# Places of the q, k, v weight buffers in SBUF: k-blocks padded to 1280 and 1536 bytes, operands of TensorE at multiples of 256 bytes

## The chip, the cores and the metric

The kernel runs on one core of a Trainium2 chip. The metric is the device time of one execution in microseconds; the median of several runs is compared. A profile is one more execution, taken by the hardware profiler. It has its own span (first to last instruction) and its own time.

## The reference

x has S = 2048 rows of D = 640. After a layer norm, xn goes two ways: a sliding, dilated attention (32 heads of 20, a window of 8 positions at distance 2), and a bilinear feed-forward part with F = 1536. The output is x plus the product of both, the second one through a SiLU.

```python
qkv = xn @ wqkv                                   # 640 x 1920
idx = pos[:, None] - (arange(8) * 2)[None, :]     # positions s, s-2, ..., s-14
logits = where(idx >= 0, q . k[idx], -1e9) * 20 ** -0.5
s = (softmax(logits) . v[idx]) @ wo               # 640 x 640
g = silu(((xn @ w_gate) * (xn @ w_up)) @ w_down)  # 640 x 1536, 640 x 1536, 1536 x 640
out = x + s * g
```

## The kernel before

Matrix products keep float32 accuracy by splitting each operand into a high part (rounded to TensorE's fp32r) and a low part (the rest), and adding three products: high by high, high by low, low by high. A split (function `split`, lines 84 to 87) is a copy on ScalarE that makes the high part (line 86) and a subtraction on GpSimd or VectorE that makes the low part (line 87).

SBUF buffers are made by `st(shape, tag, bufs)`. All buffers of a tag share the same one to four places, sized by the largest; places follow one another in the order in which tags are first used, each at a multiple of 32 bytes. `skip(n)` takes n bytes and does nothing else: it only shifts what comes after it.

First half, up to about 554 us of the span. The 2048 rows are 16 tiles of 128; the normed and transposed x (`xc`, high and low, four chunks of 512 columns) stays in SBUF. Two kinds of work alternate on TensorE in an order written out by hand:

- `qkv(u, i)` (line 317): a unit u is one group of heads (5, 5, 5, 5, 6, 6) and one of the two residues of the dilation, so 12 units of 8 tiles. A call has 15 matmuls: 5 k-blocks, three times. A tile of x is the stationary operand, a k-block of the group's q, k, v weights the moving one: 3 × 100 = 300 columns for the groups of 5 heads, 3 × 120 = 360 for those of 6. Weights of a group are loaded into `wraw` and split into `wqh` and `wql` by `split_wq`, one place each for all groups. ScalarE evicts k and v into `kv` (line 319) and q into `q` (line 320). At the end of tiles 4 and 7, SP copies rows of kv from each partition to the next (line 324), the halo that the window needs.
- `gate_up(f, ch)` (line 96, by `mm3`): for 128 columns of w_gate and w_up and a chunk of 512 rows, 15 matmuls of 512 columns each into the PSUM tiles g and u. Here x is the moving operand and the weights, split into `wf`, are the stationary one. ScalarE evicts g (line 420), VectorE multiplies u by it into hs (line 431), SP stores hs (line 435).

VectorE does the attention of a unit (`attention`): products q by k (line 351) and reductions (line 354) for pairs of positions, a softmax (lines 358 to 367, the exponential on ScalarE at 363), products with v (line 372), sums (line 380), a last sum into o (line 383) that SP stores (line 388). These are put between the evictions by a budget (`advance`), so the order on VectorE is fixed when the program is built. The queues of all engines run in order; SP's queue issues all DMAs.

Second half: the products with wo (lines 96 and 789) and w_down (line 660) with 320 moving columns each, by a scheme with seven products in place of eight. The places of wqh, wql, q, kv and xc are used again here for weights, inputs and results. Between the halves lies a stretch in which VectorE and GpSimd prepare those operands (lines 491, 698 to 701, 744 to 747, 764, 768).

Places modulo 256 bytes that matter, from the program's table: t, xc, wf, gs, hs, ident start at 0; q and kv at 160; wqh at 192; wql at 224. Inside xc and wf, operands start at multiples of 512. Inside wqh and wql the k-blocks lie 1200 or 1440 bytes apart.

Of the kernel before, what the change touches and what calls it, by code (L numbers as in the profile page):

```python
# [12 lines left out]
F32R = mybir.dt.float32r  # L13
# [6 lines left out]
P = 128  # L20
# [6 lines left out]
KD, KF = D // P, F // P  # L27
# [24 lines left out]
def kernel(  # L52
# [23 lines left out]
    def st(shape, tag, bufs, dt=F32):  # L76
        cnt[0] += 1
        return sb.tile(shape, dt, tag=tag, bufs=bufs, name=f"{tag}_{cnt[0]}")
# [5 lines left out]
    def split(eng, raw, hi, lo):  # L84

        nc.scalar.activation(hi, raw, AF.Copy)  # L86
        eng.tensor_sub(lo, raw, hi.bitcast(F32))  # L87
# [10 lines left out]
    def skip(n):  # L98

        cnt[0] += 1  # L100
        sb.tile([P, n // 4], F32, tag=f"skip_{cnt[0]}", bufs=1, name=f"skip_{cnt[0]}")


    wq_raw, wq = {}, {}
# [10 lines left out]
    def split_wq(g, eng, ks=(0, KD)):  # L115
        c3 = 3 * GROUPS[g] * DH
        if g not in wq:
            wq[g] = st([P, KD, c3], "wqh", 1, F32R), st([P, KD, c3], "wql", 1, F32R)
        for k0, k1, t in wq_raw[g]:
            if ks[0] <= k0 < ks[1]:  # L120
                split(eng, t, wq[g][0][:, k0:k1], wq[g][1][:, k0:k1])
# [172 lines left out]
    def begin_unit(u):  # L294
        g, r = UN[u]
        c = GROUPS[g] * DH
        q_t[u] = st([P, NE, c], "q", 2)
        if r not in kv_buf:
            kv_buf[r] = st([P, EXT * 2 * CMAX], "kv", 2)
            kv_zero[r] = 0  # L300
        kv_t[u] = kv_buf[r][:, :2 * EXT * c].rearrange("p (a e c) -> p a e c", a=2, c=c)
        if kv_zero[r] != GROUPS[g]:
            nc.gpsimd.memset(kv_t[u][0:1, :, 0:W - 1, :], 0.0)
            kv_zero[r] = GROUPS[g]
# [499 lines left out]
            nc.sync.dma_start(s_scr[2 * p + 1], yb)  # L804


    skip(192)
    begin_unit(0)
    skip(192)
    mask = st([1, NE, W], "mask", 1)  # L810
    nc.gpsimd.memset(mask, 0.0)
    for i in range(NE - 1):
# [10 lines left out]
    norm(0, 1, cuts=(0, 2 * P, D))  # L823
    mv1 = moments(1, 1)
    split_wq(0, nc.gpsimd, (0, 2))
    trans(0, parts=((0, 2), (2, KD)), later=True)
    low_parts(1)
    norm(1, 1, mv1)
    low_parts()
    split_wq(0, nc.gpsimd, (2, 4))  # L830
    split_wq(0, nc.vector, (4, KD))
    load_x(12, 1, xa[:, 0:1])
    mv2, mv3 = moments(2, 1), st([P, 1, 2], "mv", 3)
# [297 lines left out]
```

## Time and profile before

| | |
|---|---|
| median of 3 runs | 778.97 us (778.11 to 779.29) |
| profiled execution, its time | 780.43 us |
| profiled execution, its span | 778.6 us |
| granted TensorE clock, mean | 0.995 |
| TensorE matmuls in the trace | 4408 |
| of these, line 317 with 300 and 360 columns | 960 and 480 |

Times in the profile are us from the span's start unless marked ns. PE is TensorE's matmuls, PEld its weight loads, DVE is VectorE, ACT is ScalarE, POOL is GpSimd, SP issues DMAs. In a view of the timeline a row has the start, the length, the engine, the line, the operation, out<-in by the program's names, the shape and how many instructions were merged into the row; in brackets stands the idle time of the engine before it and what ended that. A merged row of matmuls is longer than the matmuls' distance times their number, because the last one's tail is in it; the pace is read from start to start. The rows of the chain of waits have start, length and what. In a view of groups, "x12 | 8.9, 740 | 21.5" is 12 instructions, 8.9 us busy, 740 ns mean, 21.5 us of idle time before them.

### The profile page before, as it was taken

The page shows a single profiled execution, that of the slowest core. Times are in us where ns is not written, and L with a number is a line of the kernel's source. Part 1 is how long each engine was busy: PE and PEld are TensorE (multiplying, and loading weights), DVE is VectorE, ACT ScalarE, POOL GpSimd, SP SyncE. Part 2 cuts the span into 40 slices and gives each one's busy share as a digit, 9 for nine tenths or more (in the row PEclk, how much of TensorE's full clock was granted, in tenths as well). Part 3 has the DMA queues.
Part 4 walks back from the last instruction along what each step waited for, and adds up shares of the span by engine and source line. Part 5 has one row for each costly group of instructions (what it writes and reads, how often), then busy time and mean ns, then how long its engine had stood idle before and what let it go on. Part 6 is the DMA issues. An engine that isn't in the chain of part 4 may idle for free.

```text
span 778.6 us, 11229 instructions
## 1 busy us (share of the span) xinstructions
PE 767.9 (99%) x4408; PEld 707.5 (91%) x4408; DVE 697.3 (90%) x731; ACT 235.2 (30%) x537; POOL 150.1 (19%) x114
## 2 busy tenths in 40 slices
PE   8999999999999999999999999999899999999997
PEld 7989899898989898989898989888799999999997
DVE  7899899999999999997999999999986787777775
ACT  4324312031112121312121212113455564444442
POOL 5200401022023101210204010034456720000000
PEclk9999999999999999999999999999999999999999
DMA  8552131321224122333032231444467674555533
GB/s 325 168 191 77 49 90 44 96 90 48 85 50 124 49 64 82 98 83 79 29 108 70 60 88 50 128 123 104 138 191 227 205 264 162 198 188 183 183 102 135
DMA packets 82252, 93.97 MB, mean 121 GB/s; under 512 B 23112, under 2 KB 63384, under 8 KB 82072
## 3 DMA queue, kind: packets, MB, share of 16 engines
q1 hardware_dynamic: 82200, 93.27, 38.7%
q8 instruction: 34, 0.56, 0.3%
q14 instruction: 18, 0.15, 0.1%
HBM read 55.84 MB, written 28.31 MB: 108 GB/s over the span
## 4 chain that ended last, share of the span: by engine, by line
PE 67%; DVE 24%; issue 5%; DMA 1%; ACT 1%; POOL 1%; DVEq 0%; SPq 0%; ACTq 0%; POOLq 0%
PE q L317 19%; PE q L660 11%; PE u L96 10%; PE g L96 10%; PE u L660 5%; PE q L96 5%; DVE t L351 4%; DVE t L380 4%; DVE t L372 4%; PE g L660 3%; DVE lg L354 2%; PE q L789 2%; DVE hs L431 2%; DVE xc L221 1%; PE u L789 1%
## 5 line engine op out<-in xcount | busy, mean ns | idle before, releaser
L96 PE MATMUL u<-xc,wf 128*128 128x512 f32 (+1 forms) x735 | 171.9, 386 | 0.4 <-DVE hs L431 0.4
L96 PE MATMUL g<-xc,wf 128*128 128x512 f32 (+1 forms) x735 | 172.1, 386 | 0.0
L317 PE MATMUL q<-wqh,xc 128*128 128x300 f32 (+1 forms) x960 | 161.6, 312 | 0.3
L96 PEld LDWEIGHTS u<-xc,wf 128*128 128x128 f32 x735 | 136.0, 188 | 28.0 <-DVE hs L431 0.8
L96 PEld LDWEIGHTS g<-xc,wf 128*128 128x128 f32 x735 | 135.7, 188 | 26.7
L317 PEld LDWEIGHTS q<-wqh,xc 128*128 128x128 f32 x960 | 147.0, 189 | 2.6 <-ACT wqh L86 0.4
L351 DVE TENSOR_TENSOR t<-q,kv 128x1600 f32<-128x1600 f32 (+1 forms) x48 | 98.7, 2055 | 6.2 <-DMA kv<-kv 6.2
L87 POOL TENSOR_TENSOR wf<-wraw,wf 128x256 fp32r<-128x256 f32 (+2 forms) x22 | 47.6, 2183 | 266.4 <-ACT wf L86 229.4
L372 DVE TENSOR_TENSOR t<-e,kv 128x1600 f32<-128x1600 f32 (+1 forms) x48 | 97.7, 2053 | 1.1
L354 DVE TENSOR_REDUCE lg<-t 128x80 f32<-128x1600 f32 (+1 forms) x48 | 92.6, 1929 | 1.1
L317 PE MATMUL q<-wql,xc 128*128 128x300 f32 (+1 forms) x480 | 87.2, 312 | 0.0
L420 ACT ACTIVATE gs<-g 128x512 f32<-128x512 f32 x48 | 28.6, 597 | 192.5 <-PE g L96 175.9
L380 DVE TENSOR_TENSOR t<-t,t 128x1600 f32<-128x1600 f32 (+1 forms) x36 | 78.8, 2190 | 1.0
L317 PEld LDWEIGHTS q<-wql,xc 128*128 128x128 f32 x480 | 75.4, 191 | 0.0
L319 ACT ACTIVATE kv<-q 128x200 f32<-128x200 f32 (+1 forms) x96 | 33.4, 348 | 125.2 <-PE q L317 125.2
L660 PE MATMUL q<-xc,wf 128*128 128x320 f32 x432 | 67.2, 309 | 0.0
L87 POOL TENSOR_TENSOR wql<-wraw,wqh 128x300 fp32r<-128x300 f32 (+4 forms) x14 | 35.3, 2539 | 165.6 <-ACT wqh L86 165.4
L660 PEld LDWEIGHTS q<-xc,wf 128*128 128x128 f32 x432 | 64.3, 188 | 0.0
L431 DVE TENSOR_TENSOR hs<-u,gs 128x512 f32<-128x512 f32 x47 | 32.0, 681 | 0.0
L87 POOL TENSOR_TENSOR xc<-wraw,xc 128x320 fp32r<-128x320 f32 (+1 forms) x22 | 26.2, 1193 | 28.5 <-ACT xc L86 25.4
L320 ACT ACTIVATE q<-q 128x100 f32<-128x100 f32 (+1 forms) x96 | 24.9, 259 | 0.0
L623 DVE TENSOR_TENSOR wf<-t,wf 128x768 fp32r<-128x768 f32 x16 | 15.3, 956 | 8.2 <-ACT wf L619 7.5
(259 smaller groups left out, 913.0 us busy)
## 6 DMA issues: line engine op xcount, KB each, us to landing
h_scr<-hs SPq DMA_DIRECT2D x48, 256.0 KB, 2.2
wraw<-in_wgu SPq DMA_DIRECT2D x12, 640.0 KB, 5.1
t<-h_scr SPq DMA_DIRECT2D x8, 768.0 KB, 7.0
hs<-s_scr SPq DMA_DIRECT2D x16, 320.0 KB, 3.5
gs<-in_x SPq DMA_DIRECT2D x16, 320.0 KB, 4.0
out<-q SPq DMA_DIRECT2D x14, 320.0 KB, 2.7
wraw<-h_scr SPq DMA_DIRECT2D x11, 384.0 KB, 5.9
wraw<-in_wd SPq DMA_DIRECT2D x12, 320.0 KB, 3.8
```

The costliest lines, as they stand in the source:

```text
L87: eng.tensor_sub(lo, raw, hi.bitcast(F32))
L96: nc.tensor.matmul(acc, a, b, start=first and n == 0, stop=last and n == len(runs) - 1)
L317: nc.tensor.matmul(p, xT[(r * NE + i) // TPC][a][:, k, t0:t0 + P], wq[g][b][:, k], start=n == 0, stop=n == len(runs) - 1, skip_group_check ...
L319: nc.scalar.activation(kv_t[u][:, :, W - 1 + i, :], p[:, c:].rearrange("p (a c) -> p a c", a=2), AF.Copy)
L320: nc.scalar.activation(q_t[u][:, i, :], p[:, :c], AF.Copy)
L351: nc.vector.tensor_mul(t, q.rearrange("p i c -> p (i c)").unsqueeze(1).to_broadcast([P, 2, NE * c]), places(0, j))
L354: nc.vector.tensor_reduce(out=lg[:, :, j:j + 2].rearrange("p n a -> p a n"), in_=heads(t), op=ALU.add, axis=AX.X)
L372: nc.vector.tensor_mul(heads(t), pw, heads(places(1, j)))
L380: nc.vector.tensor_add(acc, acc, t)
L420: nc.scalar.activation(gs, pp[0], AF.Copy)
L431: nc.vector.tensor_mul(hs, pp[1], gs)
L660: nc.tensor.matmul(p, y[:, i, k], wd_t[name][k][:, l], start=new and r == 0, stop=r == len(runs) - 1, skip_group_check=True)
```

## The change

The high and low buffers of the q, k, v weights get rows of k-blocks padded to a multiple of 64 columns: 320 (1280 bytes) for 300 used columns and 384 (1536 bytes) for 360. The used part of each block is a slice. Two of the skipped stretches are made smaller, so that what follows starts elsewhere.

```diff
     def split_wq(g, eng, ks=(0, KD)):
         c3 = 3 * GROUPS[g] * DH
         if g not in wq:
-            wq[g] = st([P, KD, c3], "wqh", 1, F32R), st([P, KD, c3], "wql", 1, F32R)
+            cols = -(-c3 // 64) * 64
+            wq[g] = [st([P, KD, cols], tag, 1, F32R)[:, :, :c3] for tag in ("wqh", "wql")]
         for k0, k1, t in wq_raw[g]:
...
-    skip(192)
+    skip(32)
     begin_unit(0)
-    skip(192)
+    skip(160)
     mask = st([1, NE, W], "mask", 1)
```

With it q, kv, wqh and wql start at 0 modulo 256, and so does every k-block; t, xc, wf, gs, hs and ident still start at 0. Of TensorE's operands only sel (three small matmuls) and own stay at other multiples of 64. The two weight buffers grow from 7200 to 7680 bytes each. The instructions and their order on every engine are the same as before; ten copies on ScalarE and ten subtractions on GpSimd write two or three separated pieces where they wrote one run.

## The prediction

> **What bounds the kernel now.** I read the page first, then busy time by stage, then the chain of waits, and at last the timeline around the places where the chain changes engine.
>
> ```profile
> span 778.6 us, 11229 instructions
> ...
> PE 767.9 (99%) x4408; PEld 707.5 (91%) x4408; DVE 697.3 (90%) x731; ACT 235.2 (30%) x537; POOL 150.1 (19%) x114
> ```
>
> ```profile
> 130.00:371.10 241.10, 240.73 (x1327) 216.60 (x1326) 227.98 (x163) 47.77 (x135) 38.29 (x13) 1.00 0.28 77
> 371.10:490.00 118.90, 118.90 (x623) 108.60 (x622) 116.73 (x74) 23.07 (x64) 18.69 (x6) 1.00 0.24 69
> 490.00:556.90 66.90, 64.66 (x288) 53.47 (x286) 65.55 (x53) 14.33 (x22) 22.38 (x10) 1.00 0.47 130
> 562.70:774.00 211.30, 211.30 (x1440) 211.00 (x1439) 163.43 (x211) 103.81 (x198) 43.42 (x42) 1.00 0.56 186
> ```
>
> The numbers after each stretch are its length, then busy time of PE, PEld, DVE, ACT and POOL. From 130 to 557 us TensorE and VectorE are both full; after 562.7 TensorE alone is. In the stretch where both are full, the one that makes the other wait sets the time, and that is seen where the stretch ends:
>
> ```profile
> 553.61 1.04 PE L789 MATMUL q<-wf,kv 128*128 128x320 f32 x6
> ...
> 556.29 0.68 DVE L431 TENSOR_TENSOR hs<-u,gs 128x512 f32<-128x512 f32 x1
> ...
> 557.03 1.15 PE L789 MATMUL u<-xc 128*128 128x320 f32 x6 [2.38 <-DVE hs L431]
> ...
> 559.23 1.82 PE L789 MATMUL q<-xc 128*128 128x320 f32 x6 [1.05 <-ACT o L792]
> ...
> 560.85 0.47 PE L789 MATMUL u<-wqh,xc 128*128 128x320 f32 x1
> ...
> 564.39 0.32 PE L789 MATMUL g<-wqh,kv 128*128 128x320 f32 x1
> ```
>
> At 557.03 TensorE has been idle for 2.38 us because VectorE was behind with an eviction (hs, line 431). So TensorE arrives 2.38 us early, and VectorE's queue sets the moment from which the TensorE-bound rest (557 to 774) counts. Then 1.05 us more are lost, and for about 14 matmuls a single one shows 0.47 us where it shows 0.32 later: the clock is down.
>
> VectorE itself waits only once between 131 and 557 us for more than 0.6 us:
>
> ```profile
> 364.04 0.99 DVE L383 TENSOR_TENSOR o<-t 128x800 f32<-128x800 f32 x1
> ...
> 364.92 0.37 ACT L319 ACTIVATE kv<-q 128x240 f32<-128x240 f32 x1 [1.95 <-PE q L317]
> 365.06 0.99 SPq L388 DMA_DIRECT2D o_scr<-o  x2
> ...
> 366.14 1.59 SPq L324 DMA_DIRECT2D kv<-kv  x2
> ...
> 371.19 4.03 DVE L351 TENSOR_TENSOR t<-q,kv 128x1920 f32<-128x1920 f32 x1 [6.16 <-DMA kv<-kv]
> ```
>
> It waits 6.16 us for the halo copies of unit 8's k and v. What those copies wait for matters here. ScalarE has the last piece ready at 365.29 (364.92 + 0.37), but SP's queue holds the store of o first, and o was made by VectorE, ending at 365.03. The copies go out at 366.14. So TensorE is about 0.85 us ahead at this place too.
>
> **The change part by part.** No instruction is added, removed or moved on any engine: wqh and wql get padded rows of k-blocks (five blocks of 320 or 384 columns, 300 or 360 of them used), and q, kv, wqh and wql start at other places. Counted from the table of places of the two programs, modulo 256 bytes, q and kv go from 160 to 0, wqh from 192 and wql from 224 to 0, and the k-blocks, which stepped by 1200 or 1440 bytes, now all start at 0. Five costs follow.
>
> *1. Matmuls over wqh and wql (line 317).* Grouped by form, 960 have 300 columns and 480 have 360 (the mean of one holds a modelled tail and isn't the pace):
>
> ```profile
> L317 PE MATMUL q<-wqh,xc 128*128 128x300 f32 x640 | 102.8, 304 | 0.3
> ...
> L317 PE MATMUL q<-wqh,xc 128*128 128x360 f32 x320 | 58.7, 328 | 0.0
> L317 PE MATMUL q<-wql,xc 128*128 128x300 f32 x320 | 55.6, 304 | 0.0
> L317 PE MATMUL q<-wql,xc 128*128 128x360 f32 x160 | 31.7, 328 | 0.0
> ```
>
> Pieces of the chain give the pace, start to start:
>
> ```profile
> 308.01 16.62 PE q L317 x120
> ...
> 328.05 3.40 PE u L96 x15
> ...
> 345.05 19.84 PE q L317 x120
> ...
> 642.31 5.28 PE q L660 x36
> ```
>
> 512 columns: 3.40/15 = 226.7 ns; 320 columns: 5.28/36 = 146.7 ns. Both have moving operands at multiples of 256. The slope is 80.0/192 = 0.4167 ns per column and 13.3 ns are fixed. By that line 300 columns should take 138.3 ns and 360 columns 163.3. Measured: 16.62/120 = 138.5 and 19.84/120 = 165.3. So today's odd places may cost 0.2 ns for each 300-column matmul and 2.0 ns for each 360-column one, or the odd column counts do and the places nothing. One pair of rows separates place from column count:
>
> ```profile
> 763.83 2.51 PE L660 MATMUL u<-kv,wf 128*128 128x320 f32 x16
> ...
> 766.18 2.80 PE L660 MATMUL q<-xc,wf 128*128 128x320 f32 x18
> ...
> 768.82 2.80 PE L660 MATMUL g<-xc,wf 128*128 128x320 f32 x18
> ```
>
> Moving blocks in kv start at 160 modulo 256, those in xc at 0. From 763.83 to 766.18, 16 matmuls over kv: 146.9 ns each. From 766.18 to 768.82, 18 over xc: 146.7. A start at 160 costs at most 0.2 ns here. The bounds: a gain of 960 × 0.2 + 480 × 2.0 = 1.2 us, and, if the aligned blocks did as badly again as the odd 360-column ones do now, a loss of 1440 × 2.0 = 2.9 us. I take a gain of 0.5 us of TensorE time, between nothing (the kv rows) and 1.2. On the path it is worth about nothing: all but the first 300-column calls lie in the stretch where TensorE is ahead, and the wait at 557 becomes 2.9 us instead of 2.38. A loss would be swallowed likewise up to 2.38 us; of 2.9, some 0.5 would show.
>
> The Trainium skill, "SBUF — State Buffer", section "SBUF: two separate sides", says that what costs is crossing from one 16-byte line to the next. Every start and row length here is a multiple of 16 bytes before and after, so by it no pace changes and the sum keeps 0 instead of 0.5 us; the kv rows agree, the 2.0 ns at 360 columns stay unexplained by it.
>
> *2. VectorE's reads of q and kv at new places.*
>
> ```profile
> 342.95 1.81 DVE L351 TENSOR_TENSOR t<-q,kv 128x1600 f32<-128x1600 f32 x1
> ...
> 354.76 1.81 DVE L380 TENSOR_TENSOR t<-t,t 128x1600 f32<-128x1600 f32 x1
> ```
>
> The first reads q at 160 modulo 256, the second only buffers at multiples of 256: 1.81 us both. Taken as nothing; a hundredth of a us is what the rows resolve, and from 371 to 557 some 32 such products (four units, four times two) run, so ±0.3 us.
>
> *3. Splits of wqh and wql, which now write 3 or 2 separated pieces instead of one run (lines 86 and 87).*
>
> ```profile
> 538.11 1.58 POOL L87 TENSOR_TENSOR q<-wraw,q 128x640 fp32r<-128x640 f32 x1 [1.05 <-ACT q L86]
> ...
> 543.48 1.56 POOL L87 TENSOR_TENSOR xc<-wraw,xc 128x640 fp32r<-128x640 f32 x1 [3.80 <-ACT xc L86]
> ```
>
> ```profile
> L286 ACT ACTIVATE xc<-ot 128x640 fp32r<-128x640 f32 x12 | 8.9, 740 | 21.5 <-DVE ot L283 21.5
> ...
> L86 ACT ACTIVATE wqh<-wraw 128x640 fp32r<-128x640 f32 x1 | 0.7, 725 | 0.0
> ```
>
> The first POOL row writes 640 elements in one run, the second in two pieces of 320: 1.58 and 1.56 us. ScalarE writes five pieces in 740 ns, one run in 725. Ten splits: nothing on POOL, 10 × 15 ns = 0.15 us on an engine that is 30% busy. Uncovered, that delays TensorE by no more than it is ahead.
>
> *4. Halo copies of kv.* Same bytes, same packets; the start in kv moves by 160 bytes. The copies before 371 us are the only ones on the path.
>
> ```profile
> kv<-kv SPq DMA_DIRECT2D x4, 315.0 KB, 3.2
> ```
>
> Median 3.2 us to landing. Taken as nothing, bounds ±0.2 us (6% of it). The Trainium skill, "DMA: Bandwidth & Descriptors", section "How a descriptor splits into AXI transactions", says that a transfer not starting at a multiple of 256 bytes fetches from the boundary below. The copy of rows 5 to 7 of a 120-column unit starts at 32 (k) and 64 (v) modulo 256 before and at 128 and 160 after, so each 1440-byte piece grows from 46 or 47 beats to 49 or 50: an estimate by that page is 6% more transfer time, against the change.
>
> *5. The second half (products over padded wqh, wql and moved kv, q).* 320-column blocks; by the kv and xc rows the same pace at both places: nothing.
>
> Sum: the profiled execution took 780.43 us, 1.83 more than its span of 778.6, and lies 1.46 above the median of 778.97. The path loses 0 to 0.1 us (the 300-column calls before 130 us, at 0.2 ns). From 778.97 that is **778.9 us**.
>
> **The rivals.** Both come from one thing that this change can shift, the moment at which POOL's splits meet VectorE's queue.
>
> ```profile
> 404.38 2.16 DVE L380 TENSOR_TENSOR t<-t,t 128x1920 f32<-128x1920 f32 x1
> ...
> 406.81 7.94 POOL L87 TENSOR_TENSOR wql<-wraw,wqh 128x1080 fp32r<-128x1080 f32 x2 [32.17 <-ACT wqh L86]
> ...
> 408.77 4.35 DVE L380 TENSOR_TENSOR t<-t,t 128x1920 f32<-128x1920 f32 x1
> ...
> 417.33 3.32 POOL L87 TENSOR_TENSOR wf<-wraw,wf 128x1280 fp32r<-128x1280 f32 x1 [2.58 <-ACT wf L86]
> ...
> 417.87 2.15 DVE L354 TENSOR_REDUCE lg<-t 128x96 f32<-128x1920 f32 x1
> ```
>
> Beside a POOL split the product at 408.77 takes 4.35 us instead of 2.16. The reduction at 417.87, beside another split, takes its usual 2.15. POOL starts when TensorE and ScalarE get there; VectorE's position is its own. If TensorE gains or loses a us against VectorE, a split can fall on a reduction instead of a product, or the reverse, at 2.2 us each.
>
> *Slower by a split that loses its free place.* The split at 417.33 starts while a product (415.69 to 417.84) runs and then has the reduction beside it. It decides when the split comes 1.6 us earlier than VectorE's order has it now, or about as much later: it then holds up a product by 2.2 us, all on the path, since VectorE sets 557. That gives 778.9 + 2.2 = **781.1 us**. For it: VectorE is full there. Against: TensorE's shift at this place is 0.24 us (one unit of 120 × 2.0 ns) by my upper bound.
>
> *Faster by the reverse.* The split at 406.81 comes to lie beside a reduction: 2.2 us less, **776.7 us**. The wait at 557 shrinks to 0.2 us; if the clock then stays up, 14 × 0.12 = 1.7 us more, 775.0. Against it, the same smallness of the shift.
>
> *The change doesn't do what it says*, or place costs nothing and the 360 columns themselves do: line 317 keeps 165.3 ns, the time stays 779.0. This isn't told from my forecast by the total, only by the pace.
>
> **How the numbers follow.** Forecast, with the case of no effect in it: 0.58, with a range of its own from 777.9 to 780.0 (terms 2 and 4, and ±0.5 us by which the runs shown lie apart). Faster by the splits: 0.19 around 776.7. Slower by the splits: 0.19 around 781.1. Something that no row here prices, evenly on both sides: 0.04. The range from 776.6 to 781.3 takes in the middle of both rivals and leaves out about 0.17. A measurement of this kernel tells 0.2% (1.6 us) from no change: faster 0.23, same 0.53, slower 0.24.
>
> **What would show it.** Right: 360-column calls at 163.3 to 165.3 ns and 300-column ones at 138.3 to 138.5 in the chain, products at 1.81 us, TensorE's wait before 557 at 2.4 to 3.5 us, VectorE's order of long and short products as now. Wrong: any pace of line 317 outside 138 to 140 or 163 to 168 ns; kv copies later than about 5 us after issue at 366; a VectorE product that has lost or gained 2 us beside a split between 371 and 557 us; no wait at 557, which would mean that TensorE sets the time there after all.

## The result and the profile after

| | before | changed |
|---|---|---|
| median (runs) | 779.04 us (11) | 781.8 us (11) |
| lowest to highest | 777.99 to 781.88 us | 779.65 to 784.28 us |
| profiled execution, its time and span | 780.43 and 778.6 us | 781.8 and 779.9 us |

The ratio is 1.0033, 95% interval 1.0021 to 1.0045: slower by 1.6 to 3.5 us. The time lies 0.5 us above the stated range, and 0.7 us above the rival that was put at 781.1 us.

The page of the changed kernel, and its chain of waits with start, length and what:

```profile
span 779.9 us, 11229 instructions
...
PE 765.7 (98%) x4408; PEld 704.0 (90%) x4408; DVE 699.3 (90%) x731; ACT 234.8 (30%) x537; POOL 147.0 (19%) x114
```

```profile
306.37 16.40 PE q L318 x120
...
326.17 3.40 PE u L96 x15
...
343.17 19.20 PE q L318 x120
```

Line 317 is line 318 here. The 300-column matmuls take 16.40/120 = 136.7 ns (138.5 before) and the 360-column ones 19.20/120 = 160.0 ns (165.3 before); 512 columns stay at 226.7. TensorE is therefore relieved of 960 × 1.8 + 480 × 5.3 = 4.3 us, and the kernel is slower all the same. The next rows, from the timeline of the changed kernel, show what the 4.3 us turned into:

```profile
521.08 5.28 PE L96 MATMUL u<-xc,wf 128*128 128x512 f32 x15 [2.50 <-DVE hs L432]
...
557.17 1.14 PE L790 MATMUL u<-xc 128*128 128x320 f32 x6 [2.74 <-DVE hs L432]
...
559.37 1.97 PE L790 MATMUL q<-xc 128*128 128x320 f32 x6 [1.06 <-ACT o L793]
...
561.13 0.47 PE L790 MATMUL u<-wqh,xc 128*128 128x320 f32 x1
...
565.72 0.31 PE L790 MATMUL g<-wqh,kv 128*128 128x320 f32 x1
```

There is a new wait of 2.50 us at 521.08 for an eviction by VectorE, and the old one before 557 is longer (2.74 against 2.38). TensorE restarts at 557.17, where it was 557.03. The fifteen matmuls behind the new wait take 5.11 us to the start of the next call at 526.19, instead of 3.40; the clock granted from 521 to 527 us is 0.72 there and 1.00 before. After the old wait the matmuls show 0.47 us until about 565 instead of 562.7; the clock granted from 555 to 570 us is 0.77, and 0.89 before.

Why VectorE isn't earlier shows near 460 us. First the kernel before, then the changed one, VectorE and GpSimd in the timeline:

```profile
463.28 2.15 DVE L351 TENSOR_TENSOR t<-q,kv 128x1920 f32<-128x1920 f32 x1
464.36 3.89 POOL L87 TENSOR_TENSOR wf<-wraw,wf 128x1280 fp32r<-128x1280 f32 x1 [43.71 <-ACT wf L86]
465.35 0.68 DVE L431 TENSOR_TENSOR hs<-u,gs 128x512 f32<-128x512 f32 x1
465.95 2.14 DVE L354 TENSOR_REDUCE lg<-t 128x96 f32<-128x1920 f32 x1
```

```profile
458.66 2.15 DVE L355 TENSOR_REDUCE lg<-t 128x96 f32<-128x1920 f32 x1
460.45 2.94 POOL L87 TENSOR_TENSOR wf<-wraw,wf 128x1280 fp32r<-128x1280 f32 x1 [42.36 <-ACT wf L86]
460.73 4.68 DVE L352 TENSOR_TENSOR t<-q,kv 128x1920 f32<-128x1920 f32 x1
```

Before, the split starts 1.08 us into a product, which goes on undisturbed; the split stretches to 3.89 us and has the eviction and the reduction beside it. In the changed kernel it starts 0.28 us before the product is due, and the product takes 4.68 us instead of 2.15. The split came 3.9 us earlier (464.36 to 460.45), as TensorE and ScalarE reached it earlier; the product came only 2.55 us earlier. The Trainium skill, "SBUF — State Buffer", section "SBUF: two separate sides", says that GpSimd and a VectorE operation with two SBUF inputs share one pair of ports as an exclusive lock, and whichever starts first keeps it for the whole instruction. The rows agree: the split ends at 463.39, and 2.02 us later, about a product's own length, the product ends.

The profiled execution of the kernel before was slower to start: the same matmul (u<-xc,wf with 256 columns, four in a row) begins at 27.31 us in it and at 25.83 us in the changed kernel's. So times of the two are compared over a stretch: from VectorE's first product of unit 8 to TensorE's restart between the halves.

| kernel | first product of unit 8 | restart | stretch | product beside the split near 460 us |
|---|---|---|---|---|
| before | 371.19 | 557.03 | 185.8 | 2.15 |
| changed | 368.97 | 557.17 | 188.2 | 4.68 |
| e1, padding alone | 369.07 | 555.53 | 186.5 | 2.15 |
| e2, q and kv moved alone | 369.30 | 555.58 | 186.3 | 2.15 |
| e5, that split 1.3 us later | 369.58 | 555.75 | 186.2 | 2.15 |

### The profile page after: what moved, and what is told of

It is laid out like the page before. It is cut to its first block, busy times and chain, and to the rows that moved or that the text cites. A ratio compares the mean times of both kernels' runs of the same rounds, so it can differ in the third digit from the quotient of the medians.

```text
span 779.9 us, 11229 instructions
## 1 busy us (share of the span) xinstructions
PE 765.7 (98%) x4408; PEld 704.0 (90%) x4408; DVE 699.3 (90%) x731; ACT 234.8 (30%) x537; POOL 147.0 (19%) x114
## 4 chain that ended last, share of the span: by engine, by line
PE 68%; DVE 22%; issue 5%; DMA 2%; ACT 1%; POOL 1%; SPq 0%; DVEq 0%; ACTq 0%; POOLq 0%
PE q L318 19%; PE u L96 11%; PE g L96 11%; PE q L661 11%; PE u L661 5%; PE q L96 5%; DVE t L381 4%; DVE t L373 4%; DVE t L352 4%; PE g L661 3%; PE q L790 2%; DVE lg L355 2%; DVE hs L432 1%; PE u L790 1%; DVE xc L222 1%
## 5 line engine op out<-in xcount | busy, mean ns | idle before, releaser
L96 PE MATMUL u<-xc,wf 128*128 128x512 f32 (+1 forms) x735 | 173.9, 388 | 3.1 <-DVE hs L432 2.9
L318 PE MATMUL q<-wqh,xc 128*128 128x300 f32 (+1 forms) x960 | 158.3, 307 | 0.5 <-DVE xc L289 0.3
L318 PEld LDWEIGHTS q<-wqh,xc 128*128 128x128 f32 x960 | 144.4, 188 | 2.8 <-DVE xc L289 0.5
L373 DVE TENSOR_TENSOR t<-e,kv 128x1600 f32<-128x1600 f32 (+1 forms) x48 | 100.4, 2109 | 1.1
L318 PE MATMUL q<-wql,xc 128*128 128x300 f32 (+1 forms) x480 | 85.2, 307 | 0.0
L381 DVE TENSOR_TENSOR t<-t,t 128x1600 f32<-128x1600 f32 (+1 forms) x36 | 80.8, 2245 | 1.0
L318 PEld LDWEIGHTS q<-wql,xc 128*128 128x128 f32 x480 | 73.6, 188 | 0.0
L364 ACT ACTIVATE e<-lg 128x320 f32<-128x320 f32 (+1 forms) x12 | 5.9, 489 | 64.2 <-DVE lg L362 64.2
```

What stands on the lines that cost most here:

```text
L96: nc.tensor.matmul(acc, a, b, start=first and n == 0, stop=last and n == len(runs) - 1)
L318: nc.tensor.matmul(p, xT[(r * NE + i) // TPC][a][:, k, t0:t0 + P], wq[g][b][:, k], start=n == 0, stop=n == len(runs) - 1, skip_group_check ...
L373: nc.vector.tensor_mul(heads(t), pw, heads(places(1, j)))
L381: nc.vector.tensor_add(acc, acc, t)
```

## The experiments

**e1 and e2: the two halves of the change.** e1 pads the k-blocks, with q and kv at 160 modulo 256. e2 moves q and kv alone.

```diff
-    skip(32)
+    skip(192)
     begin_unit(0)
-    skip(160)
+    skip(256)
```

> The padded k-blocks at multiples of 256 bytes, but q and kv back at 160 modulo 256 as before. Theory T (the pace of TensorE on line 318 does it: TensorE gains about 4 us, runs further ahead of VectorE, and the split of f = 9 meets a product instead of a reduction): 360-column matmuls at 160 ns and 300-column ones at 137 ns as in the changed kernel, one long product of 4.7 us near 460 us, time as the changed kernel, about 781.8 us. Rival R (the new places of q and kv slow VectorE, ScalarE or the halo copies): time back near 779.0 us.

Measured: 781.58 us, ratio 1.0031 (1.0019 to 1.0042), as slow as the whole change. But its profiled execution was the fastest of its six (780.03; the others 781.4 to 782.4) and has no long product, against what was expected. Its timeline:

```profile
460.38 4.98 POOL L87 TENSOR_TENSOR wf<-wraw,wf 128x1280 fp32r<-128x1280 f32 x1 [42.60 <-ACT wf L86]
460.39 2.15 DVE L352 TENSOR_TENSOR t<-q,kv 128x1920 f32<-128x1920 f32 x1
```

The two start 0.01 us apart, and here VectorE won. In the profiles of e4 and e3 below the split starts 0.03 and 0.07 us ahead of the same product; there GpSimd won, and the product took 4.93 and 4.90 us. Whether it went that way in the other five of e1 wasn't seen, since they have no profile. The times of the changed kernel fall apart in the same way, three of 779.65 to 780.05 us and eight of 781.23 to 784.28; that the same race decides between them is likely, but not shown.

e2 is the kernel before with these skips:

```diff
-    skip(192)
+    skip(32)
     begin_unit(0)
-    skip(192)
+    skip(352)
```

> q and kv at 0 modulo 256, wqh and wql unpadded at their old places. Theory T: line 317 keeps 138.5 and 165.3 ns, time as before, 779.0 us within 0.6. Rival R: as slow as the changed kernel, about 781.8 us.

Measured: 779.57 us, ratio 1.0002 (0.9994 to 1.0011), with 16.62 and 19.84 us for 120 matmuls of line 317 as before. The places of q and kv cost nothing that shows within that interval; the rival R falls.

**e3 and e5: the split that lost its free place, made later.** In the changed kernel, ScalarE's copy is done twice for one set of weights.

```diff
         for k0, k1 in zip(cuts, cuts[1:]):
+            if f == 9:
+                nc.scalar.activation(hi[:, k0:k1], wf_raw[f][:, k0:k1], AF.Copy)
             split(eng, wf_raw[f][:, k0:k1], hi[:, k0:k1], lo[:, k0:k1])
```

> The changed kernel with ScalarE's copy of the weights of f = 9 done twice, so that POOL's split near 460 us starts about 1.3 us later, inside a product that already runs. Theory T: the product of 4.68 us there goes back to about 2.15 us, VectorE is 2.5 us earlier from there on, TensorE's wait before 557 us shrinks from 2.7 us to under 1 us, time 779 us or less (778 to 779.5). Rival R, or a loss made after 557 us alone (rival G, the clock gate): the long product goes but the time stays within 1 us of 781.8.

Measured: 782.41 us (ratio 1.0044, 1.0027 to 1.0062). I had miscounted: f = 9 is the split near 414 us. It starts at 414.94 (414.10 in the changed kernel), and the product at 460.5 us still took 4.90 us. So this leaves the theory untested; it shows only that a second copy on ScalarE for another split wins nothing. e5 has `f == 10`.

> Mends e3, which delayed the split before the one meant: here ScalarE's copy of the weights of f = 10 is done twice, and POOL's split that meets the long product near 460 us starts about 1.3 us later, inside a product that already runs, and then has hs and a reduction beside it. Theory T (this split's lost free place makes VectorE late at 557 us): product at 460 us back to about 2.2 us, restart after the wait between the halves 2 us earlier than the changed kernel's 557.2 for a like start, time 779.6 us (779.0 to 780.2). Rival G (the lowered clock after the waits alone): time within 0.6 us of 781.8.

Measured: 779.65 us, ratio to before 1.0004 (0.9994 to 1.0014). The timeline of e5:

```profile
460.59 2.15 DVE L354 TENSOR_TENSOR t<-q,kv 128x1920 f32<-128x1920 f32 x1
461.96 3.60 POOL L87 TENSOR_TENSOR wf<-wraw,wf 128x1280 fp32r<-128x1280 f32 x1 [44.00 <-ACT wf L86]
462.66 0.68 DVE L434 TENSOR_TENSOR hs<-u,gs 128x512 f32<-128x512 f32 x1
463.26 2.15 DVE L357 TENSOR_REDUCE lg<-t 128x96 f32<-128x1920 f32 x1
```

More work on ScalarE (1.28 us) takes 2.15 us off the median. None of the twelve times of e5 is above 780.02 us. The restart, at 555.75, comes 1.4 us earlier than in the changed kernel for a like start. That is less than the 2 us expected: the product near 460 us has its 2.5 us back, but in e5 another product, at 527.51, loses 1.24 us to a split. The split of f = 10 has its free place back, and nearly the whole loss is gone.

**e4 and e6: the clock kept up through the wait.** Five products of the identity are put on TensorE where it idles between the halves, on the changed kernel (e4) and on the one before (e6).

```diff
     pair_product(0, 0)
+    warm = pt([P, 3, P], "q", 4)
+    busy(warm, 4)
...
         pair_product(p, 1)
+        if p == 0:
+            busy(warm, 1)
```

> The changed kernel with five idle products of the identity (about 0.64 us each) on TensorE where it waits between the halves: four before the wait of 2.7 us, one before the wait of 1.1 us. Rival G (the time is lost by the lowered clock after these waits, 22 matmuls at 120 ns each instead of 14 before): the matmuls after 559 us run at 147 ns, time 779.2 us (2.6 us less). Theory T (VectorE is late by 557 us): the clock part is only the difference of 22 to 14 matmuls, 1 us, but all 2.6 us can be won here too; TensorE still restarts at about 557 us. If the time stays at 781.8, the clock costs nothing on the path.

> The kernel before with the same five idle products as e4. If the lowered clock after the waits costs the kernel before as much as the changed one, this wins some 1.7 to 2.5 us (777.0 to 777.8) and the clock explains little of the difference between the two: then changed and before differ by 2 us with the clock kept up on both, which is VectorE's lateness (theory T). If rival G holds, this stays at 779.5, as fast as e4.

Measured: e4 779.58 us (ratio to before 1.0007, 0.9998 to 1.0016), 2.2 less than the changed kernel; e6 777.53 us, ratio 0.9980 (0.9968 to 0.9992), 1.4 to 2.0 less than the kernel before, whose median was 778.97 us beside e6 and 779.5 beside e4. Timeline of e4:

```profile
554.04 2.74 PE L174 MATMUL q<-ident 128*128 128x384 f32 x8
556.89 1.15 PE L795 MATMUL u<-xc 128*128 128x320 f32 x6
...
560.08 0.31 PE L795 MATMUL u<-wqh,xc 128*128 128x320 f32 x1
```

The matmuls after the wait take 0.31 us at once, and the clock granted from 555 to 570 us is 1.00. The lowered clock costs the changed kernel 2.2 us and the kernel before 1.4 to 2.0, so by the medians it explains at most 0.8 us of their difference: with the clock up on both, they still lie 2.05 us apart. In the two profiled executions its share is somewhat larger: from the restart to the end of the span the changed kernel takes 222.7 us and the kernel before 221.6. But e2, with the same granted clock of 0.77 there as the changed kernel, was as fast as the kernel before. Rival G falls as the main cause; the clock is a cost of both kernels, and its exact share in their difference stays open.

**e7, e8, e9: does TensorE's gain come out when VectorE has less to do?** The low parts of wql for all groups but the first are made by VectorE itself, on the changed kernel (e7) and on the one before (e8).

```diff
-    split_wq(1, nc.gpsimd)
+    split_wq(1, nc.vector)
...
-            split_wq(UN[u + 1][0], nc.gpsimd)
+            split_wq(UN[u + 1][0], nc.vector)
```

> The changed kernel with the low parts of wql made by VectorE itself for all groups but the first (five pairs of subtractions, about 1.7 to 2.0 us a pair at one element per 1.04 ns), where POOL's splits held VectorE's products up by 3.0 to 3.8 us a pair. VectorE's queue gets shorter by some 1.3 us three times before 371 us and 1.6 us once after it. Theory T (TensorE has some 4 us to spare that VectorE hides): restart 4 to 5 us earlier, time 775 to 777.5 us, and 2 to 4 us under e8. Rival G: gains no more than e8 does.

> The same edit on the kernel before. VectorE's queue gets shorter by the same 4 to 5 us, but TensorE has only 2.4 us to spare there: its wait before 557 us goes, the clock stays up, time 775.5 to 777.5 us and bounded by TensorE from then on. Theory T: e7 is faster than this by 2 to 4 us, by what line 318 gains.

Measured: e7 773.42 us (ratio 0.9932, 0.9909 to 0.9955), e8 774.71 us (0.9938, 0.9920 to 0.9956). Both win more than expected; e7 is only 1.3 us faster than e8, not 2 to 4. The timeline of e8, then of e7, says why:

```profile
406.25 2.09 DVE L87 TENSOR_TENSOR wql<-wraw,wqh 128x1080 fp32r<-128x1080 f32 x2
...
551.49 1.04 PE L789 MATMUL q<-wf,kv 128*128 128x320 f32 x6
552.62 1.14 PE L789 MATMUL u<-xc 128*128 128x320 f32 x6
```

```profile
458.26 2.95 POOL L87 TENSOR_TENSOR wf<-wraw,wf 128x1280 fp32r<-128x1280 f32 x1 [42.29 <-ACT wf L86]
459.06 4.17 DVE L352 TENSOR_TENSOR t<-q,kv 128x1920 f32<-128x1920 f32 x1
...
550.22 1.14 PE L790 MATMUL u<-xc 128*128 128x320 f32 x6 [2.36 <-DVE hs L432]
```

On VectorE a pair of subtractions takes 2.09 us, where a pair on GpSimd cost VectorE 3.6 us (in the kernel before, 4.35 for 2.16 at 408.77 and 2.60 for 1.16 at 413.16). In e8 the restart comes 1.13 us after the six matmuls ahead of it began, which need 0.88 (6 × 0.147): a wait of 0.25 us, so TensorE is all but setting the time there, and what it could gain would show. In e7 the split of f = 10 met a product again, and TensorE waits 2.36 us. e9 is e7 with the late split of e5.

> e7 with the late split of e5 as well: in e7 VectorE still set the restart between the halves (wait 2.4 us), with 2.0 us lost at the split of f = 10. Theory T: that loss goes, the wait before the restart falls under 1 us, TensorE's gain on line 318 comes out, time 770 to 772.5 us, below e7 (773.4) and e8 (774.7). If VectorE has another limit there: within 0.7 us of e7.

Measured: 770.66 us, ratio to before 0.9900 (0.9884 to 0.9916). The chain and the timeline of e9:

```profile
341.36 19.20 PE q L320 x120
```

```profile
547.20 1.04 PE L792 MATMUL q<-wf,kv 128*128 128x320 f32 x6
548.36 1.14 PE L792 MATMUL u<-xc 128*128 128x320 f32 x6
```

Of the wait before the restart some 0.3 us are left (1.16 less 0.88). e9 is 4.05 us faster than e8, and its restart comes 4.26 us earlier (548.36 against 552.62), close to the 4.3 us that line 318 gains. It beats both kernels of this case, by 8.4 and 11.1 us.

**e10 to e12: which places count.** The buffers stay where the changed kernel has them; only the k-blocks' distance and first place differ. The diff is that of e10; e11 has `-(-c3 // 16) * 16, 0`, and e12 `-(-c3 // 64) * 64, 8` in a buffer of 2048 columns.

```diff
-            cols = -(-c3 // 64) * 64
-            wq[g] = [st([P, KD, cols], tag, 1, F32R)[:, :, :c3] for tag in ("wqh", "wql")]
+            cols, at = c3, 0
+            wq[g] = [st([P, KD * 384], tag, 1, F32R)[:, at:at + KD * cols].rearrange("p (k c) -> p k c", c=cols)[:, :, :c3]
+                     for tag in ("wqh", "wql")]
```

> The changed kernel's buffers with k-blocks not padded (1200 and 1440 bytes apart, starting at 0 modulo 256, then at 176, 96, 16, 192 or at 160, 64, 224, 128). Read from line 318's pace: 138 to 139 and 165 ns on the mean if starts off 64 bytes cost, whichever base; 137 and 160 ns if only the base of the buffer mattered.

> k-blocks at multiples of 64 bytes (1216 and 1472 apart), at 0, 64, 128 and 192 modulo 256. If 64 bytes are the unit: 137 and 160 ns for every block. If 256 bytes are: the blocks at 0 at 160 ns, the others above, mean about 164.

> k-blocks 1280 and 1536 bytes apart as in the changed kernel, all shifted by 32 bytes, so every start is at 32 modulo 256. If equal starts of all blocks are what counts: 137 and 160 ns. If the place within 64 bytes counts: a constant pace above, near 139 and 163 to 166 ns.

The 360-column calls in the chains of e10, e11 and e12, one fence each:

```profile
345.03 19.69 PE q L319 x120
```

```profile
343.27 19.68 PE q L319 x120
```

```profile
343.43 19.73 PE q L319 x120
```

That is 164.1, 164.0 and 164.4 ns each, where the changed kernel has 160.0. Multiples of 64 bytes don't do it, nor an aligned buffer alone, nor equal starts at 32 modulo 256; starts that are all multiples of 256 do. Multiples of 128 weren't tried. Whether each block's own start decides isn't shown. From one matmul's start to the next, the block at 0 has 159 ns in e10 and the others 164 to 167. But in e11, which was expected to have its blocks at 0 at 160 ns, these have 167 and 164, and the others 162 to 165. In e12, where all starts are alike, the distances go 168, 161 and 164 in turn, so a single distance can't be read as the price of its block. Each of the three was run once: 780.43, 779.23 and 778.94 us. The split near 460 us kept its free place in all three.

## Why the prediction was wrong

- **Term 1, the matmuls over wqh and wql: the step that failed.** I drew a line through 320 and 512 columns, took it as the pace that aligned blocks could at best reach (138.3 and 163.3 ns), and set the gain between 0 and 1.2 us, taking 0.5. It is 4.3 us: with all blocks aligned the matmuls are faster than that line (136.7 and 160.0), so the line was no lower bound. The kv rows, which I read as showing that a start at 160 costs nothing, were a control for 320 columns only, that is for rows of exactly 5 × 256 bytes.
- **Where the gain goes: right in kind.** I held that VectorE sets the restart and a gain of TensorE would turn into waiting. It did: 2.50 us at 521, where I expected no wait, and 2.74 us at 557 against 2.38. e9 gets the gain back once VectorE is out of the way. What I had wrong is that this is all it does: I put the gain's effect on the path at nothing, and it also moved a split.
- **The rival that came true, at another split.** The price of 2.2 us was near (2.5 at the product, 2.4 over the stretch). I placed it at 417 us and gave it 0.19, since by my bound TensorE's shift there was 0.24 us and 1.6 were needed. (Two units of 360 columns lie before that place, at 345.05 and 385.33 in the chain, so the bound should have been 0.48; still too little.) With the true gain the split near 464 us moved 3.9 us and VectorE's product 2.55; these 1.36 us between them were more than the 1.08 us that the split had to spare. The mis-sized term 1 made the rival look unlikely. The time came out above the rival's as well, since it has no term for a longer lowered clock: in the two profiled executions, counted from the like matmul near 26 us, VectorE's unit 8 starts 0.7 us earlier, the stretch to the restart is 2.4 us longer and the rest 1.2 us longer, 2.8 us in all, where the medians differ by 2.76.
- **Terms 2, 4 and 5: right.** Products on VectorE keep 2.15 us (456.47 in the changed kernel's timeline reads the same as 463.28 before), e2 as a whole is at 1.0002, and the second half runs at 146.7 ns. The halo copies of 315 KB land in 3.3 us at the median, 3.2 before, which lies within the ±0.2 us. TensorE was ahead at the halo copies of unit 8 in the changed kernel too: the store of o goes out first.

```profile
362.33 0.99 DVE L384 TENSOR_TENSOR o<-t 128x800 f32<-128x800 f32 x1
362.41 0.37 ACT L320 ACTIVATE kv<-q 128x240 f32<-128x240 f32 x1 [1.87 <-PE q L318]
...
363.35 0.99 SPq L389 DMA_DIRECT2D o_scr<-o  x2
...
364.43 1.60 SPq L325 DMA_DIRECT2D kv<-kv  x2
```

- **Term 3: right.** The separated pieces cost nothing that shows: GpSimd's splits of 360-column blocks at 403 to 410 us hold VectorE up by 3.6 us, as the unbroken ones did.
- **What would prove it wrong** was named and seen: paces of line 317 outside 138 to 140 and 163 to 168 ns, and a product that lost 2 us beside a split.

## What to carry to other kernels

When two engines run full side by side, making one faster does nothing by itself, but it moves every point at which their work meets; look for the places where a third engine's instruction has a free slot by less than the shift. A few tenths of a us decide there, so such places are worth pinning down (a later copy, the work on another engine) before the faster version is judged. A control measurement shows that a placement is free only for the row length that it was made with.

## What the runs showed of the hardware

- The fp32r matmuls of 300 and 360 columns take 136.7 and 160.0 ns where all moving operands start at multiples of 256 bytes. With k-blocks that aren't padded (e10 and the kernel before), with starts at multiples of 64 bytes (e11) or at a constant 32 modulo 256 (e12), the 360-column ones take 164.0 to 165.3 and the 300-column ones 137.9 to 138.5. For 320 columns, starts at 160 and at 0 modulo 256 both take 147 ns. Why the row length matters wasn't tried.
- By the rule of 16-byte lines that the prediction takes from the Trainium skill, "SBUF — State Buffer", section "SBUF: two separate sides", these places would be alike. The pace differs by 4 to 5 ns of 160, so that rule alone doesn't give it here.
- A few hundredths of a us decide which of GpSimd and VectorE goes first: with the split 0.03 us ahead (e4) the product took 4.93 us, with 0.01 us between them (e1) VectorE won and the product took 2.15. Each was seen in one execution.
